# Second MoE: the slot table with 128 columns side by side per chunk

## The chip, the cores and the metric

The kernel runs on one core of one Trainium2 chip. The metric is the device time in microseconds (us) of one launch. The instructions run on five engines: TensorE (PE; its weight loads are listed apart as PEld), VectorE (DVE), ScalarE (ACT), GpSimd (POOL) and SyncE (SP). Each engine takes its own instructions strictly in the order of its queue.

## The reference

The program is banded attention with a linear bias, then a first mixture of experts (MoE) that sends each token to one expert, then a second MoE. What the change touches belongs to the second:

```python
def _moe2_ref(x, w_gate, w1, w2):
    N, D = x.shape                 # 3072, 512
    E = w_gate.shape[1]            # 8
    cap = N // E                   # 384
    logits = x @ w_gate
    order = np.argsort(-logits.flatten())
    assigned = -np.ones(N, dtype=np.int64)
    counts = np.zeros(E, dtype=np.int64)
    for idx in order:
        tok, e = (int(idx) // E, int(idx) % E)
        if assigned[tok] >= 0 or counts[e] >= cap:
            continue
        assigned[tok] = e
        counts[e] += 1
    ...
    for e in range(E):
        mask = assigned == e
        out[mask] = np.maximum(x[mask] @ w1[e], 0.0) @ w2[e]
```

w1 is 512 x 1024 and w2 1024 x 512 for each expert. Each expert ends with exactly 384 tokens.

## The kernel before

Products in fp32 are made of three matmuls in fp32r on high and low parts: high x high, high x low, low x high. So each weight and each activation has a high part (names ending in h) and a low one (ending in l). In the second MoE w1 is wbh and wbl, w2 is wah and wal; xh and xl are the transposed tokens, hh and hl the hidden layer. The high parts of the weights are made on ACT (L119), the low ones on DVE (L121), each chunk of w1 as a pair of two 512-wide halves, four pairs in all, and the same for w2.

The second MoE has eight phases (`phase`, from L1079). Phase i finds the next expert that fills up and its 384 tokens:

- It walks through six digits of the sorted key, DIGITS = 64, 32, 32, 64, 64, 32. For each digit DVE compares (`count`, geT, L1123), PE sums the 0/1 table (`pick`, cg, L1134; 12 matmuls for a digit of 64, 6 for one of 32), DVE copies (cgz, L1136), PE folds (cp, L1141), DVE compares (flz, L1144), PE spreads the result over the partitions (`spread`, fp, L1150), and DVE counts (fo, L1152) and sets up the next digit (db, yk, L1156).
- It numbers the tokens that were found: the matmuls cs (L1229) and spx (L1232, L1241), then on DVE acc, sg and sm. A token's number is split into a column (col) and a row (rw, L1269).
- Four comparisons of 768 elements (L1271) make the 0/1 table `slots` of 128 rows by 24 chunks of tokens, bm and br (L1274 to L1277) make the right side, and 24 matmuls `ip` (L1281), each with one chunk's 128 rows as its stationary matrix, yield the list of tokens: icp (L1283), idx (L1285).

In `slots` the chunk is the innermost index: the 128 elements that one ip takes lie 24 f16 numbers apart.

While phase i+1 runs, expert i is computed. `weights` loads w1 as soon as the expert's number is known (SP, L116, then L119 and L121). `tokens` gathers the tokens through idx into XB (POOL, L1321) and transposes them on PE in three blocks (L151), from which come xh on ACT (L154) and xl on DVE (L155). `ffns` does layer 1 (hp, L175; hh on ACT L179, hl on DVE L180), 96 matmuls of 384 columns, then layer 2 (yp, L207), 72 matmuls of 512 columns, yo on ACT (L1359) and the scatter to the output.

The order on PE is written by `merge`: every generator yields a cost (in columns, 2.4 to the ns) and `merge` takes a matmul from `ffns` until the other generators' cost is used up. So `yield 6000` between the table and ip puts 6000 units of hp or yp there. `phases` multiplies each cost by 1.04 (0.9 in the first phase). The order on DVE, ACT and POOL is set by the compiler's scheduler.

```python
    def phases():
        yield 10000
        for i in range(E):
            while i and -2 not in done1:
                yield 100
            for w in phase(i, found[i]):
                yield (1.04 if i else 0.9) * w
```

Of the kernel before, what the change touches and what calls it, by code (L numbers as in the profile page):

```python
# [12 lines left out]
F16 = mybir.dt.float16  # L13
I32 = mybir.dt.int32
AF = mybir.ActivationFunctionType
OP = mybir.AluOpType
# [13 lines left out]
def attention_moe_moe_kernel(  # L30
# [17 lines left out]
    nc = tc.nc  # L48
# [207 lines left out]
    with ExitStack() as actx:  # L256
# [68 lines left out]
        if not dense:  # L325
# [11 lines left out]
            if n_global:  # L337
                nc.vector.memset(dist[:, G0:G0 + n_global], float(n_local))
                nc.vector.tensor_scalar(dist[:, 256:256 + n_global], dist[:, 256:256 + n_global], float(n_local), None,
                                        op0=OP.min)  # L340
# [230 lines left out]
        for n in range(B * NP):  # L571
            b, hp = divmod(n, NP)
# [66 lines left out]
            if n >= B * NP - 9 and not dense:  # L639
                c = n - (B * NP - 9)  # L640
# [53 lines left out]
    sm1 = ctx.enter_context(tc.tile_pool(name="sm1", bufs=1))  # L694
# [71 lines left out]
    NC_ = N // 128  # L766
# [249 lines left out]
    sel = ctx.enter_context(tc.tile_pool(name="sel", bufs=1))  # L1016
# [6 lines left out]
    for n in (32, 64):  # L1023
# [9 lines left out]
    above = sel.tile([E, 2, 32], F32)  # L1033
    nc.gpsimd.iota(above, pattern=[[1, 2], [1, 32]], base=0, channel_multiplier=0,
                   allow_small_or_imprecise_dtypes=True)
    slots = sm1.tile([128, 2, 128, NC_], F16, name="slots", tag="slots")
    slot16, ao = slots[:, 0], slots[:, 1]
    nc.gpsimd.iota(slot16, pattern=[[1, 128], [0, NC_]], base=0, channel_multiplier=0,
                   allow_small_or_imprecise_dtypes=True)
    pc = sel.tile([128, 1], F32)  # L1040
    nc.gpsimd.iota(pc, pattern=[[1, 1]], base=0, channel_multiplier=1, allow_small_or_imprecise_dtypes=True)
# [32 lines left out]
    def bc(ap, n):  # L1074
        return ap[:, :, None].to_broadcast([128, ap.shape[1], n])
# [4 lines left out]
    def phase(i, found):  # L1080
# [17 lines left out]
        else:  # L1098
# [63 lines left out]
            for a_, sh in enumerate((10, 4, 0)):  # L1162
                nc.vector.tensor_scalar(ki[:, 3 + a_], key, 0xFFFF, sh, op0=OP.bitwise_and,
                                        op1=OP.logical_shift_right)
# [39 lines left out]
            for i_ in range(2):  # L1204
                cx = sel.tile([E, 32], F32, name="cx")
                nc.vector.scalar_tensor_tensor(cx, above[:, i_], dgs[0:E, 5:6], cp[:, :32], op0=OP.is_equal,
                                               op1=OP.mult, accum_out=ct[:, i_:i_ + 1])
            nc.vector.scalar_tensor_tensor(fdz[0:E], ct[:, 1:2].to_broadcast([E, E]), rem8, dcode,
                                           op0=OP.is_ge, op1=OP.mult)
# [51 lines left out]
        sm = sel.tile([128, NC_], F32, name="sm")  # L1261
        nc.vector.tensor_add(sm, sg[:, 0], sg[:, 1])
        nc.vector.tensor_scalar(sm, sm, -1.0, None, op0=OP.add)
        col = sel.tile([128, NC_], F32, name="col")
        nc.vector.tensor_scalar(col, sm, 128.0, None, op0=OP.is_ge)
        for i_ in range(2, NB2):
            nc.vector.scalar_tensor_tensor(col, sm, 128.0 * i_, col, op0=OP.is_ge, op1=OP.add)
        rw = sel.tile([128, NC_], F16, name="rw")
        nc.vector.scalar_tensor_tensor(rw, col, -128.0, sm, op0=OP.mult, op1=OP.add)  # L1269
        for r0 in range(0, 128, 32):  # L1270
            nc.vector.tensor_tensor(ao[:, r0:r0 + 32], slot16[:, r0:r0 + 32],  # L1271
                                    rw[:, None, :].to_broadcast([128, 32, NC_]), op=OP.is_equal)
        bm = sel.tile([128, NC_, NB2], F16, name="bm")
        nc.vector.tensor_tensor(bm, bc(col, NB2), colv[:, None, :].to_broadcast([128, NC_, NB2]), op=OP.is_equal)  # L1274
        br = sel.tile([128, NC_, 2, NB2], F16, name="br")
        nc.vector.tensor_scalar(br[:, :, 0], bm, pc, None, op0=OP.mult)
        nc.vector.tensor_mul(br[:, :, 1], bm, bc(cv, NB2))  # L1277
        yield 6000
        ip = ps.tile([128, 2, NB2], F32, name="ip", tag="sp")
        for c in range(NC_):  # L1280
            nc.tensor.matmul(ip, ao[:, :, c], br[:, c], start=(c == 0), stop=(c == NC_ - 1))  # L1281
        icp = sel.tile([128, NB2], F32, name="icp")
        nc.vector.tensor_copy(icp, ip[:, 1])  # L1283
        idx = sel.tile([128, NB2], I32, name="idx", bufs=E)
# [7 lines left out]
# [7 lines that stand above are left out]
# [98 lines left out]
```

## Time and profile before

| | |
|---|---|
| median of 3 runs | 985.92 us |
| lowest and highest | 983.97 and 986.55 us |
| the profiled execution's own time | 986.66 us |
| its span in the profile | 984.9 us |
| mean granted clock of PE | 0.979 |
| busy: PE, DVE, ACT, POOL | 94%, 56%, 43%, 30% |

The span runs from the first to the last instruction of the profiled execution; the time of the execution holds 1.8 us more. The second MoE fills the last third. Its phases end with ip at 625, 669, 712, 755, 799, 842, 884 and 901 us, so a period of the steady part lasts some 43 us. The phase that ends at 712 us is phase 2, counted from 0.

### The profile page before, as it was taken

The numbers are of one execution on the slowest core, as the hardware profiler recorded it, in microseconds if no ns is written. First come the engines' busy times: TensorE is split into PE (matmuls) and PEld (weight loads), VectorE is DVE, ScalarE is ACT, GpSimd is POOL, SyncE is SP. The second block draws the span as 40 slices with busy tenths as digits, with TensorE's granted clock in tenths as the row PEclk, the third lists the DMA queues.
The fourth block names the chain that finished last, engine by engine and source line by source line (L and its number), as shares of the span: only waits on it lengthen the run. The fifth ranks groups of instructions, "written<-read, shape, count | busy, mean of one in ns | idle before, by whom it ended". The sixth has DMA issues, their size and how long they took to land.

```text
span 984.9 us, 17460 instructions
## 1 busy us (share of the span) xinstructions
PE 927.5 (94%) x6253; PEld 773.4 (79%) x6253; DVE 556.2 (56%) x1928; ACT 424.5 (43%) x939; POOL 298.5 (30%) x272
## 2 busy tenths in 40 slices
PE   7999999999987999999999989689999999998997
PEld 6877777776886899899797756587868787787996
DVE  6657676676232443433334345877878688784530
ACT  5887878875233433334234320134333333432430
POOL 3111534241135465463623871301020210103001
PEclk9999999999998999999999999889999999998999
DMA  8999855630364446544441411515244261524510
GB/s 162 203 200 198 209 140 140 135 124 33 97 195 168 147 134 203 154 141 126 143 150 65 129 52 42 207 51 204 97 150 150 87 213 48 201 101 165 177 39 32
DMA packets 124192, 133.24 MB, mean 135 GB/s; under 512 B 83445, under 2 KB 83585, under 8 KB 124097
## 3 DMA queue, kind: packets, MB, share of 16 engines
q1 hardware_dynamic: 114449, 105.96, 38.6%
q0 software_dynamic: 9648, 26.09, 8.2%
q8 instruction: 51, 0.84, 0.4%
q14 instruction: 44, 0.36, 0.1%
HBM read 103.77 MB, written 28.23 MB: 134 GB/s over the span
## 4 chain that ended last, share of the span: by engine, by line
PE 47%; DVE 8%; issue 7%; DMA 5%; POOL 3%; ACT 1%; POOLq 0%; ACTq 0%; SPq 0%; DVEq 0%
PE hp L175 21%; PE yp L207 12%; PE yp L191 7%; DMA raw<-in_moe_w_dram 4%; DVE wal L121 4%; PE hp L151 2%; PE ip L1281 1%; POOL lg_dram L86 1%; POOL wbl L121 1%; PE cg L1134 1%; DVE geT L1123 1%; DMA XB<-x_dram,idx 1%; ACT wah L119 1%; DVE wbl L121 1%; POOL out_dram L86 1%
## 5 line engine op out<-in xcount | busy, mean ns | idle before, releaser
L179 ACT ACTIVATE hh<-hp 128x384 fp32r<-128x384 f32 (+9 forms) x130 | 63.4, 489 | 186.8 <-PE hp L175 173.1
L180 DVE SCALAR_TENSOR_TENSOR hl<-hp,hh 128x384 fp32r<-128x384 f32 (+9 forms) x130 | 71.8, 554 | 112.5 <-ACT hh L179 112.1
L86 POOL DMA_INDIRECT out_dram<-yo,idx x24 | 26.2, 1091 | 255.1 <-ACT yo L1359 227.1
L121 POOL TENSOR_TENSOR wbl<-raw,wbh 128x1024 fp32r<-128x1024 f32 x28 | 66.4, 2388 | 95.8 <-ACT wbh L119 55.8
L458 ACT ACTIVATE pb<-pb,mn 128x232 f32<-128x232 f32 (+1 forms) x192 | 88.8, 465 | 15.1 <-DVE mn L456 14.5
L207 PE MATMUL yp<-wah,hh 128*128 128x512 f32 x224 | 93.0, 415 | 0.0
L121 DVE TENSOR_TENSOR wal<-raw,wah 128x512 fp32r<-128x512 f32 (+1 forms) x78 | 67.4, 903 | 45.0 <-ACT wah L119 44.5
L119 ACT ACTIVATE wbh<-raw 128x1024 fp32r<-128x1024 f32 x60 | 62.7, 1058 | 69.1 <-DMA raw<-in_moe_w_dram 64.8
L207 PE MATMUL yp<-wah,hl 128*128 128x512 f32 x224 | 91.8, 410 | 0.0
L207 PE MATMUL yp<-wal,hh 128*128 128x512 f32 x224 | 91.4, 408 | 0.0
L444 PE MATMUL sc<-kx,qd 128*128 128x232 f32 (+1 forms) x384 | 88.7, 355 | 2.5 <-POOL kx L420 1.3
L175 PE MATMUL hp<-xl,wah 128*128 128x240 f32 (+8 forms) x260 | 90.9, 349 | 0.0
L175 PE MATMUL hp<-xh,wah 128*128 128x240 f32 (+8 forms) x260 | 90.1, 346 | 0.4 <-PEq L835 0.4
L175 PE MATMUL hp<-xh,wbh 128*128 128x384 f32 (+1 forms) x260 | 90.0, 346 | 0.0
L175 PE MATMUL hp<-xh,wal 128*128 128x240 f32 (+8 forms) x260 | 89.8, 346 | 0.0
L119 ACT ACTIVATE wah<-raw 128x1024 fp32r<-128x1024 f32 x68 | 68.6, 1052 | 48.4 <-DMA raw<-in_moe_w_dram 46.9
L175 PE MATMUL hp<-xh,wbl 128*128 128x384 f32 (+1 forms) x260 | 89.4, 344 | 0.0
L175 PE MATMUL hp<-xl,wbh 128*128 128x384 f32 (+1 forms) x260 | 89.4, 344 | 0.0
L456 DVE CUSTOM_DVE_ANT_0 pb<-sc,bias_w 128x232 f32<-128x232 f32 x160 | 56.7, 393 | 32.3 <-PE sc L444 18.5
L444 PEld LDWEIGHTS sc<-kx,qd 128*128 128x128 f32 x384 | 64.3, 194 | 10.1 <-POOL kx L420 2.4
L121 POOL TENSOR_TENSOR wal<-raw,wah 128x1024 fp32r<-128x1024 f32 x22 | 58.2, 2658 | 42.2 <-ACT wah L119 27.1
L191 PE MATMUL yp<-hh,wbh 128*128 128x240 f32 (+5 forms) x192 | 65.5, 341 | 3.1 <-ACT yt L197 2.1
(307 smaller groups left out, 2140.7 us busy)
## 6 DMA issues: line engine op xcount, KB each, us to landing
raw<-in_moe_w_dram SPq DMA_DIRECT2D x128, 512.0 KB
xs_dram<-qd SPq DMA_DIRECT2D x8, 1032.0 KB
vn<-in_v_dram SPq DMA_DIRECT2D x32, 192.0 KB
kn<-in_k_dram SPq DMA_DIRECT2D x30, 192.0 KB
qn<-in_q_dram SPq DMA_DIRECT2D x30, 192.0 KB
rawg<-in_moe_w_dram SPq DMA_DIRECT2D x8, 512.0 KB
XB<-xs_dram SPq DMA_DIRECT2D x9, 241.9 KB
XB<-xs_dram SPq DMA_DIRECT2D x7, 258.0 KB
```

The lines of the kernel that those rows point to most:

```text
L86: st = nc.gpsimd.indirect_dma_start(out=dst, out_offset=bass.IndirectOffsetOnAxis(ap=idx, axis=0), in_=src, in_offset=None)
L119: nc.scalar.activation(hi, raw, AF.Copy)
L121: lo_engine.tensor_tensor(lo[:, c], raw[:, c], hi[:, c], op=OP.subtract)
L151: tr = nc.tensor.transpose(tp[:, kk], rows[:, kk * 128:(kk + 1) * 128], ident[0:nt, 0:nt])
L175: nc.tensor.matmul(hp_[:, :m], a[:, c], b_[:, kk, t], start=(i == 0), stop=(i == 3 * KD - 1))
L179: nc.scalar.activation(hh[:, t], hp_[:, :m], AF.Relu)
L180: nc.vector.scalar_tensor_tensor(hl[:, t], hp_[:, :m], 0.0, hh[:, t], op0=OP.max, op1=OP.subtract)
L191: nc.tensor.matmul(yp, a[:, c], b_[:, :n], start=(f == 0 and i == 0), stop=(f == KF - 1 and i == 2))
L207: last_mm[0] = nc.tensor.matmul(yp, a[:, c], b_, start=(f == 0 and i == 0), stop=(f == KF - 1 and i == 2))
L444: nc.tensor.matmul(sc[:, h, off:], lhs, kx[:, t, off:], start=True, stop=True)
L456: nc.vector.tensor_tensor_reduce(p[:, h, off:], sc[:, h, off:], bt, 1.0, 3.0e38, OP.add, OP.min, mn)
L458: nc.scalar.activation(p[:, h, off:], p[:, h, off:], AF.Exp, bias=mn, scale=-1.0, accum_out=sums[:, t, hh:hh + 1])
```

## The change

`slots` becomes [128, 24 chunks, 8, 16]: for each chunk 128 columns side by side. The table of row numbers slot16 now holds 128 numbers (it held 128 x 24). rw is written with each row number repeated 16 times, 384 numbers in place of 24, and the comparison, still 4 instructions of 768 elements, runs over 6 chunks at a time in runs of 16 elements. ip takes its 128 columns from one contiguous stretch. The cost that is yielded ahead of ip goes from 6000 to 6500.

```diff
--- before.py
+++ after.py
@@ -1033,9 +1033,10 @@
     above = sel.tile([E, 2, 32], F32)
     nc.gpsimd.iota(above, pattern=[[1, 2], [1, 32]], base=0, channel_multiplier=0,
                    allow_small_or_imprecise_dtypes=True)
-    slots = sm1.tile([128, 2, 128, NC_], F16, name="slots", tag="slots")
-    slot16, ao = slots[:, 0], slots[:, 1]
-    nc.gpsimd.iota(slot16, pattern=[[1, 128], [0, NC_]], base=0, channel_multiplier=0,
+
+    ao = sm1.tile([128, NC_, 8, 16], F16, name="slots", tag="slots")
+    slot16 = sel.tile([128, 8, 16], F16, name="slot16")
+    nc.gpsimd.iota(slot16, pattern=[[16, 8], [1, 16]], base=0, channel_multiplier=0,
                    allow_small_or_imprecise_dtypes=True)
     pc = sel.tile([128, 1], F32)
     nc.gpsimd.iota(pc, pattern=[[1, 1]], base=0, channel_multiplier=1, allow_small_or_imprecise_dtypes=True)
@@ -1265,20 +1266,21 @@
         nc.vector.tensor_scalar(col, sm, 128.0, None, op0=OP.is_ge)
         for i_ in range(2, NB2):
             nc.vector.scalar_tensor_tensor(col, sm, 128.0 * i_, col, op0=OP.is_ge, op1=OP.add)
-        rw = sel.tile([128, NC_], F16, name="rw")
-        nc.vector.scalar_tensor_tensor(rw, col, -128.0, sm, op0=OP.mult, op1=OP.add)
-        for r0 in range(0, 128, 32):
-            nc.vector.tensor_tensor(ao[:, r0:r0 + 32], slot16[:, r0:r0 + 32],
-                                    rw[:, None, :].to_broadcast([128, 32, NC_]), op=OP.is_equal)
+        rw = sel.tile([128, NC_, 16], F16, name="rw")
+        nc.vector.scalar_tensor_tensor(rw, bc(col, 16), -128.0, bc(sm, 16), op0=OP.mult, op1=OP.add)
+        for c0 in range(0, NC_, 6):
+            cs_ = [128, 6, 8, 16]
+            nc.vector.tensor_tensor(ao[:, c0:c0 + 6], slot16[:, None].to_broadcast(cs_),
+                                    rw[:, c0:c0 + 6, None, :].to_broadcast(cs_), op=OP.is_equal)
         bm = sel.tile([128, NC_, NB2], F16, name="bm")
         nc.vector.tensor_tensor(bm, bc(col, NB2), colv[:, None, :].to_broadcast([128, NC_, NB2]), op=OP.is_equal)
         br = sel.tile([128, NC_, 2, NB2], F16, name="br")
         nc.vector.tensor_scalar(br[:, :, 0], bm, pc, None, op0=OP.mult)
         nc.vector.tensor_mul(br[:, :, 1], bm, bc(cv, NB2))
-        yield 6000
+        yield 6500
         ip = ps.tile([128, 2, NB2], F32, name="ip", tag="sp")
         for c in range(NC_):
-            nc.tensor.matmul(ip, ao[:, :, c], br[:, c], start=(c == 0), stop=(c == NC_ - 1))
+            nc.tensor.matmul(ip, ao[:, c].rearrange("p a b -> p (a b)"), br[:, c], start=(c == 0), stop=(c == NC_ - 1))
         icp = sel.tile([128, NB2], F32, name="icp")
         nc.vector.tensor_copy(icp, ip[:, 1])
         idx = sel.tile([128, NB2], I32, name="idx", bufs=E)
```

Lines of the changed kernel are one higher behind the first piece, and two higher behind ip.

The changed cost moves instructions. On PE, each later phase stands some 640 units later against layers 1 and 2: ip of phases 1 to 6 comes behind 9, 12, 15, 18, 21 and 22 yp of layer 2, where it came behind 6 each time. The transposes of the next expert's last block have 10, 7, 7, 4, 1 and 0 yp behind them before layer 1 begins (13 each time before). ACT's order moves behind stage 5 and 6 (wah behind yo and xh). SP's stays. DVE's moves at three places of each phase.

DVE in phase 4, the end of the slot table (slots are the comparisons, br the right side of ip). Before:

```order
L1274 TENSOR_TENSOR bm<-col,colv 128x72
L1114 TENSOR_SCALAR ki<-ki 128x24
L1161 TENSOR_SCALAR ki<-ki 128x24
L1115 TENSOR_REDUCE cmx<-eqb 128x24
L1161 TENSOR_SCALAR ki<-ki 128x24
L1271 TENSOR_TENSOR slots<-slots,rw 128x768 x4
L1276 TENSOR_SCALAR br<-bm,pc 128x24x3
L1277 TENSOR_TENSOR br<-bm,cv 128x24x3
```

And in the changed kernel:

```order
L1276 TENSOR_TENSOR bm<-col,colv 128x72
L1115 TENSOR_SCALAR ki<-ki 128x24
L1162 TENSOR_SCALAR ki<-ki 128x24
L121 TENSOR_TENSOR wbl_10395<-raw,wbh_10394 128x512 x2
L1116 TENSOR_REDUCE cmx<-eqb 128x24
L1162 TENSOR_SCALAR ki<-ki 128x24
L1164 TENSOR_SCALAR ki<-ki 128x24 x3
L1273 TENSOR_TENSOR slots<-slot_7652,rw 128x768 x3
L180 SCALAR_TENSOR_TENSOR hl_10365<-hp,hh_10364 128x384
L1273 TENSOR_TENSOR slots<-slot_7652,rw 128x768
L1278 TENSOR_SCALAR br<-bm,pc 128x24x3
L1279 TENSOR_TENSOR br<-bm,cv 128x24x3
```

The first pair of wbl, three ki and an hl have come to stand ahead of br.

DVE in phase 4, between br and the first digit's geT. Before:

```order
L1116 TENSOR_SCALAR db<-ki 128x24
L1163 TENSOR_SCALAR ki<-ki 128x24
L180 SCALAR_TENSOR_TENSOR hl_10347<-hp,hh_10346 128x384
L1117 TENSOR_TENSOR ohb<-codeb,cmx 128x192
L1163 TENSOR_SCALAR ki<-ki 128x24 x2
L121 TENSOR_TENSOR wbl_10394<-raw,wbh_10393 128x512 x2
L121 TENSOR_TENSOR wbl_10401<-raw,wbh_10400 128x512 x2
L1123 TENSOR_TENSOR geT<-db,jt_7643 128x1536
L121 TENSOR_TENSOR wbl_10408<-raw,wbh_10407 128x512 x2
L180 SCALAR_TENSOR_TENSOR hl_10364<-hp,hh_10363 128x384
L1165 CAST kf<-ki 128x120
```

And in the changed kernel:

```order
L121 TENSOR_TENSOR wbl_10402<-raw,wbh_10401 128x512 x2
L1117 TENSOR_SCALAR db<-ki 128x24
L1118 TENSOR_TENSOR ohb<-codeb,cmx 128x192
L1166 CAST kf<-ki 128x120
L121 TENSOR_TENSOR wbl_10409<-raw,wbh_10408 128x512 x2
L121 TENSOR_TENSOR wbl_10416<-raw,wbh_10415 128x512 x2
L1285 COPY icp<-ip 128x3
L1124 TENSOR_TENSOR geT<-db,jt_7643 128x1536
L1167 TENSOR_SCALAR yk<-kf 128x24
```

Ahead of geT there are now three pairs of wbl, kf and icp behind br, where two pairs and an hl stood.

DVE behind phase 4's table, from the last block's xl to the digit's second geT, where the low parts of w2 (wal) are made. Before:

```order
L155 TENSOR_TENSOR xl<-hp,xh 128x4x128
L121 TENSOR_TENSOR wal_10691<-raw,wah_10690 128x512 x2
L1136 CAST cgz<-cg 128x2x8
L121 TENSOR_TENSOR wal_10698<-raw,wah_10697 128x512 x2
L1144 TENSOR_SCALAR flz<-cp,rem_7680 8x64
L121 TENSOR_TENSOR wal_10705<-raw,wah_10704 128x512 x2
L1152 SCALAR_TENSOR_TENSOR fo,dgs<-fp,onef 128x64
L121 TENSOR_TENSOR wal_10712<-raw,wah_10711 128x512 x2
L1156 SCALAR_TENSOR_TENSOR db<-dgs,yk 128x24
L1156 SCALAR_TENSOR_TENSOR yk<-dgs,yk 128x24
L1123 TENSOR_TENSOR geT<-db,jt_7643 128x1536
L180 SCALAR_TENSOR_TENSOR hl_10717<-hp,hh_10716 128x384
```

And in the changed kernel:

```order
L155 TENSOR_TENSOR xl<-hp,xh 128x4x128
L121 TENSOR_TENSOR wal_10666<-raw,wah_10665 128x512 x2
L121 TENSOR_TENSOR wal_10673<-raw,wah_10672 128x512 x2
L1137 CAST cgz<-cg 128x2x8
L121 TENSOR_TENSOR wal_10680<-raw,wah_10679 128x512 x2
L1145 TENSOR_SCALAR flz<-cp,rem_7681 8x64
L121 TENSOR_TENSOR wal_10687<-raw,wah_10686 128x512 x2
L180 SCALAR_TENSOR_TENSOR hl_10692<-hp,hh_10691 128x384
L1153 SCALAR_TENSOR_TENSOR fo,dgs<-fp,onef 128x64
L1157 SCALAR_TENSOR_TENSOR db<-dgs,yk 128x24
L1157 SCALAR_TENSOR_TENSOR yk<-dgs,yk 128x24
L1124 TENSOR_TENSOR geT<-db,jt_7643 128x1536
```

cgz stands behind two pairs of wal, where it stood behind one, and an hl stands ahead of fo and geT. Behind the tables of phases 1 to 3 an hl stands ahead of geT as well; behind that of phase 5 cgz stands behind three pairs.

At the end of expert 5's layer 2, before, five yp stand between two blocks of transposes on PE and thirteen behind the last; in the changed kernel five and two, and layer 1 of expert 6 follows the last at once.

## Rows read from the trace of the kernel before

**Rows 1.** The page, part 1: busy time of an engine, its share of the span, instructions.

```profile
PE 927.5 (94%) x6253; PEld 773.4 (79%) x6253; DVE 556.2 (56%) x1928; ACT 424.5 (43%) x939; POOL 298.5 (30%) x272
```

**Rows 2.** Windows, one period: us, busy PE, PEld, DVE, ACT, POOL (x), PEclk, DMA, GB/s.

```profile
743.00:786.00 43.00, 40.97 (x283) 33.44 (x282) 33.62 (x128) 14.74 (x22) 6.32 (x6) 1.00 0.41 136
```

**Rows 3.** The chain of waits, 704 to 756 us: start, us, what.

```profile
712.26 1.66 PE ip L1281 x24
713.93 3.60 PE yp L207 x15
717.53 0.30 PE cg L1134 x12
...
729.21 0.44 PE hp L151 x4
...
731.26 0.39 DVE wal L121
...
737.83 0.46 PE cg L1134 x12
```

**Rows 4.** PE's waits, 668 to 870 us: who for whom, us in total, times, longest.

```profile
PE cg L1134 <- DVE geT L1123: 4.3, 5, 0.9
...
PE cp L1141 <- DVE cgz L1136: 1.6, 5, 0.3
```

**Rows 5.** Timeline of PE, phases 2 and 3: start, us, instruction, x count [idle <- releaser].

```profile
705.21 0.20 PE L1241 MATMUL spx<-before,csb 128*128 128x48 f16 x1
...
718.64 0.23 PE L1141 MATMUL cp<-fold,cgz 128*128 128x64 f16 x2
...
748.08 0.20 PE L1241 MATMUL spx<-before,csb 128*128 128x48 f16 x1
```

**Rows 6.** Timeline of DVE, phase 2 and the wal stretch behind it.

```profile
708.84 1.96 DVE L1271 TENSOR_TENSOR slots<-slots,rw 128x768 f16<-128x768 f16 x4
...
710.86 0.24 DVE L1277 TENSOR_TENSOR br<-bm,cv 128x72 f16<-128x72 f16 x1
...
712.06 2.49 DVE L121 TENSOR_TENSOR wbl<-raw,wbh 128x512 fp32r<-128x512 f32 x4
714.47 0.95 DVE L1123 TENSOR_TENSOR geT<-db,jt 128x1536 bf16<-128x1536 bf16 x1
...
730.35 0.69 DVE L155 TENSOR_TENSOR xl<-hp,xh 128x512 fp32r<-128x512 f32 x1
```

**Rows 7.** Groups of weight loads, 600 to 930 us: busy us, mean ns, idle before.

```profile
L1281 PEld LDWEIGHTS <-slots 128*128 128x128 f16 x192 | 13.9, 183 | 2.2 <-issue 1.9 <-DVE ki L1163 0.3
L1134 PEld LDWEIGHTS <-geT 128*128 128x128 bf16 x360 | 11.9, 97 | 17.7 <-DVE geT L1123 9.9 <-issue 4.8 <-DVE xl L155 1.4
```

**Rows 8.** Groups of DVE by form, 600 to 930 us.

```profile
L180 DVE SCALAR_TENSOR_TENSOR hl<-hp,hh 128x384 fp32r<-128x384 f32 x54 | 29.6, 549 | 8.7 <-ACT hh L179 8.6
...
L1271 DVE TENSOR_TENSOR slots<-slots,rw 128x768 f16<-128x768 f16 x32 | 15.6, 551 | 0.0
...
L1123 DVE TENSOR_TENSOR geT<-db,jt 128x768 bf16<-128x768 bf16 x20 | 11.2, 558 | 0.0
...
L1269 DVE SCALAR_TENSOR_TENSOR rw<-col,sm 128x24 f16<-128x24 f32 x8 | 1.4, 177 | 0.0
```

**Rows 9.** Timeline of SP's queue and of ACT where w1 is loaded.

```profile
619.49 12.70 SPq L116 DMA_DIRECT2D raw<-in_moe_w_dram  x8
...
623.30 1.06 ACT L119 ACTIVATE wbh<-raw 128x1024 fp32r<-128x1024 f32 x1 [36.48 <-DMA raw<-in_moe_w_dram]
...
747.64 14.21 SPq L116 DMA_DIRECT2D raw<-in_moe_w_dram  x8
```

**Rows 10.** Windows (as rows 2) and PE's timeline behind a long wait.

```profile
890.00:892.00 2.00, 2.00 (x6) 1.29 (x7) 0.08 (x1) 0.00 (x0) 1.18 (x2) 0.50 0.71 241
...
889.73 0.20 PE L1232 MATMUL spx<-stz,before 128*128 128x48 f16 x1 [2.67 <-DVE csb L1234]
...
890.33 0.63 PE L207 MATMUL yp<-wah,hl 128*128 128x512 f32 x1
```

## The prediction

> **What bounds the kernel now.** The page comes first: TensorE (PE) is busy for 94% of the span [rows 1]. That is a mean over stages, so the second view is one period of the second MoE: PE is busy for 40.97 of 43 us there, VectorE (DVE) for 33.62 [rows 2]. The third view is the chain of waits over the same period [rows 3]. It runs on PE up to 731.24 us, then for 6.5 us over DVE, along the low parts of w2 (wal) with the digit search between them, and back to PE at 737.83 with the table product cg. The fourth view, PE's waits over five periods, agrees: each time PE waits 0.9 us for geT and 0.3 for cgz [rows 4]. So a period is PE's work, plus a microsecond or so in which DVE's first-in-first-out queue is late. Two things count: what the change takes off PE, and whether it makes DVE late where it now just arrives in time.
>
> I count from the product spx at 705.21 us [rows 5], with which the slot table begins. PE is at ip at +7.05 and at the 12 matmuls cg at +12.3 [rows 3], and at cp at +13.4 [rows 5]. DVE writes the last br from +5.65 [rows 6], 1.2 us before ip can use it. Its geT starts at +9.26 and is done at +10.2 [rows 6], **2.1 us before cg needs it**.
>
> **What the change takes away.** The 24 ip matmuls hold PE for 1.66 us of the chain [rows 3]. Each takes its 128 columns out of a table in which they lie 48 bytes apart, and their weight loads last 183 ns; those of cg, whose columns lie side by side, last 97 ns [rows 7]. The twelve cg take 0.30 us [rows 3], so 24 such matmuls would take 0.60. The ends are 0.60 and, by the ratio of the loads, 1.66 x 97/183 = 0.88 us; I take 0.65, nearer to the row of whole matmuls. **PE is relieved of 1.0 us in each of 8 phases, 8.0 in all.** The Trainium skill speaks against that: TensorE: Matmul & The Clock Gate, section Weight-path perf modes — Fast Weight Load (FWL) and DoubleRow, has the fast load on whenever there are 128 weights of a type other than FP32, and ip has 128 of f16 in both kernels. By that rule ip would stay at 1.66 us, and the sum below would be 1 us higher, since only the last phase lets the gain through; rival A would fall away. The loads of 183 and 97 ns disagree with the rule.
>
> **What it adds.** rw grows from 24 to 384 numbers. The nearest row of 384 is hl with 549 ns against rw's 177 [rows 8]: **0.37 us more on DVE** in each phase (ends: nothing, if sixteen equal numbers came cheap, and 0.6). The comparison keeps its 4 x 768 elements. Its runs shrink from 24 elements to 16; geT, of 768 elements in runs of 4, takes 558 ns against 551 [rows 8], so nothing is added (ends -0.05 and +0.05 each). The smaller table of row numbers is filled by GpSimd long before its first use and costs nothing; were it late, it would show in the first comparison alone.
>
> **What it moves.** A yield of 6500 for 6000, times 1.04, shifts every later phase by 520 units against the layers, over and over, and the compiled orders follow. At phase 4 DVE now has the first pair of wbl ahead of cmx and the slots, and all four pairs, an hl and kf ahead of geT; before, two pairs and none ahead of the slots. From spx:
> - SP issues w1 0.4 us before spx (747.64 against 748.08) [rows 5, 9]. From issue to the first conversion is 623.30 - 619.49 = 3.8 us and the conversion takes 1.06 [rows 9]. So the first chunk is ready for DVE at -0.4 + 3.8 + 1.06 = +4.4; its pair of wbl, by 2.49 us for four [rows 6], ends at +5.7.
> - cmx and four ki take some 0.65 (at 0.1 to 0.26 each), the slots 4 x 0.47 (1.96 us for four, less the overlap [rows 6]), hl 0.47, two br 0.3: the last br is done at +9.0. PE stands at ip from +7.05 to +9.0, does it in 0.65, and 15 yp later is at cg at +13.2.
> - DVE meanwhile: a pair 1.25, db, ohb and kf 0.5, two pairs 2.5, geT 0.9: +14.15. **cg comes at +14.2 instead of +12.3: +1.9.** That PE was quicker at ip is lost in the wait.
>
> The other phases by the same steps:
> - Phase 0 is held by DVE from end to end: rw and two yk, **+0.5**.
> - Phases 1 and 2: no early wbl, but rw 0.37, one pair 1.25, hl 0.47 and kf 0.13 stand ahead of geT, 2.2 in all, which uses up the 2.1. Behind geT cgz waits for the last pair: **+0.6** at cp, each.
> - Phase 3 as phase 4, with hl behind the table: **+1.55**. Phase 5: **+1.6**.
> - The wal stretch [rows 3]: in phases 1 to 4 hl moves ahead of geT, **+0.47** each. In phase 5 cgz stands behind three pairs instead of one, so flz, hl and fo lose their cover: hl 0.47, the trips of flz and fo to PE and back, twice the 0.23 us that cp takes there [rows 5], and an xh behind a yo on ScalarE, 0.6 if it is as long as xl: **+1.6**.
> - Stage 6: thirteen yp stood between the last transposes and layer 1, now none. The transposes end at 729.65 in the period shown [rows 3] and xl at 731.04 [rows 6]: 1.4 us idle. With 0.4 of wait ahead of it and ip of phase 7 at -1.0: **+0.8**.
>
> **Sum:** 0.5 + 2 x (0.6 + 0.47) + (1.55 + 0.47) + (1.9 + 0.47) + (1.6 + 1.6) + 0.8 = **+11.0 us**. The profiled execution took 986.66 us, which makes 997.7; it lies 0.74 above the median of 985.92, so **997.0**. A change under 0.3%, 2.96 us, cannot be told from none, so the bounds are 983.0 and 988.9. My own range comes from the ends: rw at nothing takes off 7 x 0.37 = 2.6 and w1 landing 1 us earlier in three phases 3, so 991; ip at 0.88, w1 0.7 us later in three phases and another 1.4 at phase 5 add 4 to 5, so 1002.
>
> **Rivals.** *A, PE-bound throughout (faster).* If DVE's lateness doesn't reach PE, the 8.0 us remain: 978. For it speak PE's 94% [rows 1]; against it, that geT is already waited for in every period [rows 4] and that its 2.1 us must hold 2.2 more on DVE and the 1.0 by which PE comes earlier. It decides where fewer than two things move ahead of geT, or w1 lands before DVE has come to the slots. The Trainium skill (Perfetto Trace Analysis, section Identifying the Most-Contended Engine) says to relieve the engine with the highest occupancy first, which would have this rival win; that the chain leaves PE for 6.5 us in a period disagrees. Chance 0.14, with those cases in which part of the gain is eaten.
>
> *B, gain and delay cancel (same).* If ScalarE has the first chunk ready before DVE gets there, and hl has slack, phases 1 to 5 lose 0.2 each, phase 0 0.5, and stage 6 and 7 come out at -0.6: +0.9, 987. Chance 0.12.
>
> *C, the forecast with a lower clock (slower still).* A wait of 2.67 us is followed by a stretch in which the granted clock is 0.50 (1.2 instead of 2.4 GHz) and a yp takes 0.43 us [rows 10], where 15 take 3.6 at the full one [rows 3]: 13 of them lose 2.5. The waits of 2 us at ip and 1 at cg in phases 3 to 5 come near that; three times 2.5 is 7.5 more, 1005. Waits of 0.9 us have no such stretch behind them in the period, whose clock is 1.00 [rows 2]. Chance 0.14.
>
> *The forecast*, 991 to 1002: 0.60. **Chances:** faster 0.14, same 0.12, slower 0.60 + 0.14 = 0.74. With 2 in 10 left out, most of A and the top of C, the range goes from 984 to 1006.
>
> **What the changed profile would show.** ip in about 0.65 us with weight loads near 97 ns; rw at some 549 ns; the comparison still at 551. In phase 4 PE idle for 2 us ahead of ip, released by br, and for another 1 ahead of cg; a pair of wbl just ahead of the slots. PE's waits for geT over the five periods well over the 4.3 us of before [rows 4]. Ahead of expert 6's first hp 1.4 us idle. I am wrong if the first chunk is ready for DVE before +3.2 in phase 4, so that the slots aren't late, if geT ends before +11.3, or if ip's loads stay at 183 ns.

## Result and profile after

The changed kernel takes **990.91 us** (median of 8 runs, 988.8 to 993.31) against 984.29 us (8 runs, 981.99 to 986.55) on the same chip: ratio 1.0067, 95% interval 1.005 to 1.0083, so **slower by 6.6 us**. The forecast was 997.0 in a range of 984 to 1006, and slower. The profiled execution took 991.54 us, its span is 989.8 (984.9 before).

What the change says of itself holds. The page and the groups by form of the changed kernel, 600 to 935 us (columns as in [rows 1, 7, 8]; from the comparison on, lines are two higher than before):

```profile
PE 922.3 (93%) x6253; PEld 765.7 (77%) x6253; DVE 558.9 (56%) x1928; ACT 424.2 (43%) x939; POOL 304.5 (31%) x272
```

```profile
L1135 PEld LDWEIGHTS <-geT 128*128 128x128 bf16 x358 | 11.8, 97 | 20.9 <-DVE geT L1124 15.2 <-issue 5.0 <-DVE xl L155 0.6
L1283 PEld LDWEIGHTS <-slots 128*128 128x128 f16 x192 | 5.3, 96 | 6.6 <-DVE br L1279 5.8 <-issue 0.5 <-DVE kf L1166 0.3
```

```profile
L1273 DVE TENSOR_TENSOR slots<-slot,rw 128x768 f16<-128x768 f16 x32 | 15.8, 550 | 0.0
...
L1270 DVE SCALAR_TENSOR_TENSOR rw<-col,sm 128x384 f16<-128x384 f32 x8 | 4.4, 552 | 0.0
```

A weight load of ip takes 96 ns instead of 183 [rows 7], as one of cg does; the 24 matmuls of ip hold PE for 0.62 us, from one start to that of the next instruction, where they stood for 1.66 us in the chain [rows 3]. rw costs 552 ns instead of 177, the comparison what it did [rows 8]. PE is busy 5.2 us less, and the span is 4.9 us longer: PE waits more. Its waits, 668 to 870 us, beside [rows 4]:

```profile
PE cg L1135 <- DVE geT L1124: 5.7, 7, 1.2
PE ip L1283 <- DVE br L1279: 2.8, 3, 1.3
PE cp L1142 <- DVE cgz L1137: 2.1, 5, 0.9
PE fp L1151 <- DVE flz L1145: 1.5, 4, 0.4
PE hp L175 <- DVE xl L155: 1.3, 3, 0.7
PE hp L175 <- ACT xh L154: 1.2, 2, 0.8
```

ip, xl and xh had no wait before. Over the whole second MoE, 600 us to the end, the listed waits grow from 21.0 to 32.0 us, by 11.0; ip saves 8 x 1.05 = 8.4. The difference is 2.6 of the 4.9 us; the other 2.3 are in nothing that this view lists.

Where it happens is seen in one period, phase 4. First PE's timeline there, then DVE's:

```profile
794.77 0.20 PE L1242 MATMUL spx<-before,csb 128*128 128x48 f16 x1
...
803.89 0.76 PE L1283 MATMUL ip<-br,slots 128*128 128x6 f16 x24 [1.34 <-DVE br L1279]
...
808.91 0.46 PE L1135 MATMUL cg<-ohb,geT 128*128 128x16 bf16 x12 [0.67 <-DVE geT L1124]
```

```profile
797.66 0.55 DVE L1270 SCALAR_TENSOR_TENSOR rw<-col,sm 128x384 f16<-128x384 f32 x1
...
799.31 1.30 DVE L121 TENSOR_TENSOR wbl<-raw,wbh 128x512 fp32r<-128x512 f32 x2 [0.79 <-ACT wbh L119]
...
801.11 1.49 DVE L1273 TENSOR_TENSOR slots<-slot,rw 128x768 f16<-128x768 f16 x3
...
803.60 0.24 DVE L1279 TENSOR_TENSOR br<-bm,cv 128x72 f16<-128x72 f16 x1
803.74 1.29 DVE L121 TENSOR_TENSOR wbl<-raw,wbh 128x512 fp32r<-128x512 f32 x2
...
805.42 2.49 DVE L121 TENSOR_TENSOR wbl<-raw,wbh 128x512 fp32r<-128x512 f32 x4
...
807.90 0.95 DVE L1124 TENSOR_TENSOR geT<-db,jt 128x1536 bf16<-128x1536 bf16 x1
```

DVE stands for 0.79 us at a pair of wbl that ScalarE hasn't converted yet, with the slots queued behind it; then three pairs more go ahead of geT. The chain of waits, which in [rows 3] ran over PE in this stretch, now runs over ACT's wbh and over DVE, through wbl and the slots to geT, and meets PE at cg:

```profile
797.75 0.48 DVE rw L1270
798.23 1.06 ACT wbh L119
799.31 1.30 DVE wbl L121 x2
...
801.20 1.40 DVE slots L1273 x3
...
805.51 2.41 DVE wbl L121 x4
807.99 0.88 DVE geT L1124
808.91 0.46 PE cg L1135 x12
```

That rw released wbh is inferred by the profile, and not likely: wbh starts 3.88 us after SP issued the load of w1 here, and 3.65 to 4.44 us after it in phases 1 to 6, where the profile names other instructions or the transfer itself. More likely ACT waits for the weights, and DVE for ACT.

### The profile page after: what moved, and what is told of

The parts are those of the page before. It is cut to its first block, busy times and chain, and to the rows that moved or that the text cites. A ratio compares the mean times of both kernels' runs of the same rounds, so it can differ in the third digit from the quotient of the medians.

```text
span 989.8 us, 17442 instructions
## 1 busy us (share of the span) xinstructions
PE 922.3 (93%) x6253; PEld 765.7 (77%) x6253; DVE 558.9 (56%) x1928; ACT 424.2 (43%) x939; POOL 304.5 (31%) x272
## 4 chain that ended last, share of the span: by engine, by line
PE 40%; DVE 15%; issue 8%; DMA 5%; POOL 3%; ACT 2%; POOLq 0%; SPq 0%; ACTq 0%; DVEq 0%
PE hp L175 18%; PE yp L207 9%; PE yp L191 7%; DMA raw<-in_moe_w_dram 4%; DVE wal L121 3%; DVE wbl L121 3%; PE hp L151 2%; DVE geT L1124 1%; DVE slots L1273 1%; DVE hl L180 1%; POOL lg_dram L86 1%; POOL wbl L121 1%; PE cg L1135 1%; ACT wah L119 1%; ACT wbh L119 1%
## 5 line engine op out<-in xcount | busy, mean ns | idle before, releaser
L86 POOL DMA_INDIRECT out_dram<-yo,idx x24 | 33.4, 1390 | 278.3 <-ACT yo L1361 251.7
```

Of the source, the lines that this page charges most:

```text
L86: st = nc.gpsimd.indirect_dma_start(out=dst, out_offset=bass.IndirectOffsetOnAxis(ap=idx, axis=0), in_=src, in_offset=None)
```

## Experiments

The theory of the experiments is this. PE's gain at ip is real, and is lost because DVE's queue has the low parts of w1 (wbl) ahead of what PE waits for (slots, geT, cgz). Rival 1 is that the shift by the cost 6500 is the loss (transposes without cover), rival 2 that only the longer rw costs. Each ratio is against the kernel before on the same chip. The chips differ: the kernel before took 993.3, 996.6 and 996.8 us on those of the three groups below.

**The two halves of the change by themselves.** The new table with the old cost:

```diff
-        yield 6500
+        yield 6000
```

> The new table with the old cost 6000 ahead of ip, so the order on PE is that of before. Theory (the low parts of w1 stand ahead of geT and cgz on DVE): ip 0.62 us, but geT ends at about +12.4 after spx in phases 1 to 5 and cp comes at about +14.0 where it came at +13.4; 0.6 to 0.9 us lost in each of five phases, nothing in phase 0, 1.0 gained at the last: +2 to +3.5 us, ratio 1.002 to 1.0035. Rival 1 (the shift by 6500 is the whole loss): the 8 us of ip appear in full, 0.992. Rival 2 (only the longer rw costs): 8 less 2.6 us, 0.9945.

Measured: 1.0064 (1.0049 to 1.0079). And the old table with the new cost, the same edit the other way:

> The table of before with cost 6500 ahead of ip, nothing else. PE's order is that of the changed kernel, ip stays at 1.66 us. Theory: PE comes 0.5 us later to cg, which gives DVE slack in phases 1 and 2 (no wait for geT there); in phases 3 to 5 a pair of wbl ahead of the slots makes ip and cg wait 0.5 to 1.2 us, and the last transposes go uncovered, 1 us: +2 to +4 us, ratio 1.002 to 1.004. Rival 1 (the shift is the whole loss): +14 us, the loss of the change without its gain, 1.014. Rival 2: 1.000.

Measured: 1.0052 (1.0032 to 1.0072). Rival 1 and rival 2 both fall with the first run: PE's order is there that of before, and it is as slow as the whole change. The direction is the theory's, the size isn't: both halves cost more than forecast, and together (1.0067, on the chip of the result) they cost hardly more than each alone. The places do agree. DVE and PE in phase 2 of the run with cost 6000:

```profile
719.31 3.69 DVE L121 TENSOR_TENSOR wbl<-raw,wbh 128x512 fp32r<-128x512 f32 x6
...
723.39 0.94 DVE L1124 TENSOR_TENSOR geT<-db,jt 128x1536 bf16<-128x1536 bf16 x1
```

```profile
711.94 0.20 PE L1242 MATMUL spx<-before,csb 128*128 128x48 f16 x1
...
724.39 0.46 PE L1135 MATMUL cg<-ohb,geT 128*128 128x16 bf16 x12 [1.06 <-DVE geT L1124]
...
725.97 0.23 PE L1142 MATMUL cp<-fold,cgz 128*128 128x64 f16 x2 [0.33 <-DVE cgz L1137]
```

cg comes at +12.45 after spx and cp at +14.03, where PE's timeline of before has them at +12.16 and +13.43: the microsecond that ip gave has become a wait of 1.06, and 0.6 more is lost at cp. In the run with cost 6500 alone, phase 3 has the same picture as the change's phase 4, a wait of 0.68 us of a wbl for wbh ahead of the slots and one of 0.64 of ip for br.

**Moving wbl on DVE.** The low parts of w1 are handed out by code: two pairs are queued behind the next phase's first geT, one behind its second, one behind its third. The orders of PE, ACT and GpSimd are those of the run with cost 6000; on DVE, wbl apart, a cgz, icp or hl moves past a neighbour. (`later` holds the low parts that are not issued yet, `counts` the geT of each phase and digit; of this edit and those below only the lines that hand out are shown.)

```diff
+                for r, n_ in ((0, 2), (1, 1), (2, 1)):
+                    while (i + 1, r) not in counts:
+                        yield 100
+                    with tc.issue_after(counts[i + 1, r].ins):
+                        for _ in range(n_):
+                            later.pop(0)()
```

> The new table with cost 6000; the low parts of w1 are issued behind the next phase's digits: two pairs of wbl behind the first geT, one behind the second, one behind the third. Theory: geT ends at +8.8, cg waits for nothing and comes at +11.2, cp at +12.4, one us earlier than before; phases 1 to 5 gain 1.0 us each, the last 1.0, phase 0, which DVE bounds, 1 to 2: ratio 0.991 to 0.993. Rival 1: as its forecast for the run with cost 6000, 0.992 for both, so no difference between the two runs. Rival 2: 0.9945.

Measured: 0.9972 (0.9954 to 0.9991). The same edit on the kernel before:

> The table of before with the low parts of w1 issued behind the next phase's digits as in the run above. Theory: before, geT and cgz were just in time in phases 1 to 5, so nothing is gained there; phase 0 gains 1 to 2 us: ratio 0.998 to 0.999, and the difference to the run above is ip's 1.0 us in each phase. Rival (the order of wbl costs the same under either table): a gain as large as that between the two runs with the new table, 0.99.

Measured: 1.0012 (0.9991 to 1.0032). This pair bears the theory out: under the new table the order of wbl is worth 0.9972 - 1.0064, 8 to 9 us; under the old one nothing. The size was missed again, -2.8 where -7 to -9 us was forecast, and the two runs differ by 0.0040, half of the 8 us that the second expectation gives to ip. cg does come at +11.2 without a wait, and cp at +12.3 to +13.3, but part of the gain is handed on. PE in phase 3 of that run, and its waits from 870 us on:

```profile
755.85 0.20 PE L1249 MATMUL spx<-before,csb 128*128 128x48 f16 x1
...
767.08 0.46 PE L1142 MATMUL cg<-ohb,geT 128*128 128x16 bf16 x12
768.40 0.23 PE L1149 MATMUL cp<-fold,cgz 128*128 128x64 f16 x2
...
777.17 0.66 PE L158 MATMUL hp<-ident,XB 128*128 128x128 f32 x4 [1.80 <-DMA XB<-x_dram,idx]
```

```profile
PE spx L1240 <- DVE csb L1242: 4.2, 1, 4.2
```

In phase 3, and of the five there alone, the transposes wait for the gathered tokens, whose list idx stands behind the same wbl in DVE's queue. (The kernel before waits 0.5 us at this place, with idx at +13.4 after spx and the transposes at +20.9; here they are at +12.4 and +21.3. So idx is not later than it was: PE is ready 0.9 us sooner, and what follows idx takes longer.) Near the end spx waits longer for csb, which stands behind expert 6's wbl.

**Moving idx and csb ahead too.** wbl is queued behind idx as well, and expert 6's behind the last phase's br:

```diff
-                    with tc.issue_after(counts[i + 1, r].ins):
+                    with tc.issue_after(counts[i + 1, r].ins), tc.issue_after(idxs[i].ins):
...
+            if i == E - 2:
+                while (i + 1, 7) not in counts:
+                    yield 100
+                with tc.issue_after(counts[i + 1, 7].ins):
+                    while later:
+                        later.pop(0)()
```

> The new table with cost 6000 and the low parts of w1 behind the next phase's digits, as in the run before; they now stand behind idx as well, and those of expert 6 behind the last phase's br. Theory (the gain of the run before was handed on to waits for the gathered tokens XB, whose idx stood behind wbl, and for csb behind wbl in the last phase but one): idx at about +9 after spx in place of +13.2, no wait of the transposes for XB, no wait of spx for csb and no lower clock behind it: 4 to 8 us less than the run before, ratio 0.986 to 0.991. Rival (the gain stops because XB is late by its own transfer, whatever idx does): transposes at +20.9 after spx as before, 0.995 to 0.998.

Measured: **0.9897** (0.9863 to 0.9931), as forecast; the rival falls. idx runs at +9.4 to +10.4 after spx in phases 1 to 5, where it ran at +12.0 to +13.2 in the run before this one. PE's waits, 668 to 870 us:

```profile
PE cg L1142 <- DVE geT L1131: 3.4, 4, 0.9
PE cp L1149 <- DVE cgz L1144: 2.2, 6, 0.6
PE fp L1158 <- DVE flz L1152: 1.8, 5, 0.4
```

The wait for XB is gone, and that for csb (0.5 us are left at that spx, behind idx). The gain over the run before is thus not spread over the digits. The profiled spans are 981.6 and 989.2 us; counted from the first yp of one expert to that of the next, 2.2 us of the difference lie in phase 3, where XB was late, and 5.1 between experts 5 and 6 (37.10 instead of 42.19 us), where the wait of 4.2 us for csb was followed by some 3 us at 1.2 GHz. The kernel before has a wait there too, of 2.3 us on this chip. Against its profile on this chip, further down, the five periods of the digits give 5.7 us, this one stretch, in which ip runs twice, 5.4, and what lies ahead of them 2.0. So a good part of the gain comes from a wait that was there before the change.

**Handing out w2's low parts as well.** A pair of wal each behind the digits 4, 5 and 6 and one behind the phase's last comparison, by a generator of its own (`later2` holds the low parts of w2):

```diff
+    def lows():
+        for i in range(E - 2):
+            while i not in ready:
+                yield 100
+            for r, n_ in ((3, 1), (4, 1), (5, 1), (6, 1)):
+                while (i + 1, r) not in counts:
+                    yield 100
+                with tc.issue_after(counts[i + 1, r].ins):
+                    for _ in range(n_):
+                        later2.pop(0)()
```

> As the run with idx and br ahead of w1's low parts, and the low parts of w2 handed out too: one pair of wal behind each of the digits 4, 5 and 6 and one behind the last comparison of the phase. Theory: the waits of 0.9 us for geT, 0.3 for cgz and 0.4 for flz in the wal stretch go in each of five phases, 5 to 7 us: ratio 0.980 to 0.986. Rival (PE or the loads bound there, and wal was cover): the ratio of the run without it, to 0.002.

Measured: 0.9886 (0.985 to 0.9921), 0.001 from the run without it: the forecast failed. The waits of the wal stretch go, and as much comes back at the phase's end, where fdz now stands behind a pair of wal. PE's waits, 668 to 870 us:

```profile
PE fb L1224 <- DVE fdz L1216: 4.2, 5, 0.9
PE cp L1149 <- DVE cgz L1144: 2.6, 7, 0.8
```

The same order with the old table, and the kernel before on this chip:

> The table of before with the same order of the low parts of w1 and w2 as the run above. Theory: with DVE out of the way PE bounds, so the two differ by what ip takes less, 1.05 us in 7 or 8 phases: this run is 6 to 8 us slower than the one above, ratio 0.987 to 0.993. Rival (DVE's queue still bounds): the two are equal within 2 us.

> The kernel before, for a profile on the same chip: any theory expects 1.000, and the waits of rows 4.

Measured: 0.9905 (0.9876 to 0.9934) and 996.52 us. What the table itself is worth under this order, 0.0019 or 2.7 us by the medians, is within the intervals and less than the 6 to 8 us forecast. PE's waits for cgz are 2.6 us with the new table, as shown above, and 1.6 with the old:

```profile
PE cp L1148 <- DVE cgz L1143: 1.6, 5, 0.3
```

The periods from first yp to first yp show where ip's gain gets through. With the old table all five take 42.35 us. With the new one they take 41.44 in the two in which the first cp behind ip doesn't wait for cgz, 41.63 and 41.80 where it waits 0.06 and 0.22 us, and 42.40 where it waits 0.81. So 0.9 of ip's 1.05 us reach the period where DVE is in time, and a late cgz takes them back. The profile of the kernel before shows that chip's 10 us ahead of the second MoE's steady part: expert 0's first hp comes at 656.7 instead of 645.6 us, and cg and cp stand at +12.2 and +13.4 as ever.

**What remained open: the size.** The change and the run with cost 6000 on one chip, each with a second profile:

> The changed kernel beside the runs below, on their chip. Theory (what the cost 6500 moves on PE is worth nothing, the order of wbl on DVE everything): 1.005 to 1.008, and the run with cost 6000 within 0.003 of it. Rival (the shift itself costs): over 0.003 slower than the run with cost 6000.

> The new table with cost 6000 a second time. Theory: cgz at +13.8 after spx in phases 1 to 5 and cp at +14.0, 0.6 us later than before, the wait for geT in the wal stretch as before, idx 0.4 us later, which now and then makes the transposes wait for XB: 1.003 to 1.008. Rival (the first run fell on a disturbed stretch, the loss is the 2.5 us of cp and cg alone): 1.0005 to 1.003.

Measured: 1.0095 (1.0064 to 1.0127) for the change, above its forecast, and 1.0073 (1.0044 to 1.0102) with cost 6000, within its own. The two lie within 0.003, as the theory has it, and the intervals don't exclude that the shift costs a little. The expected later transposes are there in the second profile (+22.4 and +22.8 in phases 3 and 5 against +20.87 in the others), but XB isn't why. Windows around cg and cp of phase 5, columns as in [rows 2], and PE's timeline:

```profile
844.00:858.00 14.00, 13.83 (x94) 11.76 (x92) 13.66 (x54) 5.78 (x8) 0.00 (x0) 1.00 0.54 184
858.00:861.00 3.00, 1.78 (x19) 1.26 (x20) 2.67 (x9) 0.60 (x1) 0.00 (x0) 1.00 0.83 287
861.00:864.00 3.00, 3.00 (x10) 2.02 (x9) 1.10 (x6) 0.00 (x0) 2.28 (x3) 0.51 0.90 288
```

```profile
858.89 0.46 PE L1135 MATMUL cg<-ohb,geT 128*128 128x16 bf16 x12 [1.06 <-DVE geT L1124]
...
860.48 0.23 PE L1142 MATMUL cp<-fold,cgz 128*128 128x64 f16 x2 [0.33 <-DVE cgz L1137]
...
862.23 0.63 PE L207 MATMUL yp<-wal,hh 128*128 128x512 f32 x1
862.66 0.63 PE L207 MATMUL yp<-wah,hl 128*128 128x512 f32 x1
```

After the two waits the granted clock is 0.51 (1.2 instead of 2.4 GHz) for about 3 us, and a yp takes 0.43 us instead of 0.23. The next digit's cg comes at +18.4 after spx, where it comes at +16.9 in the phases without such a stretch: 1.55 us lost. From the first yp of expert 0 to 885 us such stretches occur once or twice in four of the five profiles of the change and its two halves (not in the change's first), twice in the run with geT first and four times in the run with a slow comparison, both below, and in no profile of the kernel before or of the runs above with w1's low parts handed out. They don't all stand behind two waits: in the change's second profile one follows a single wait of 1.49 us ahead of ip, in the run with cost 6500 alone a single one of 0.64 us. So a wait has a second price that isn't paid in every execution. The profiled execution with cost 6000 is the fastest of its six, 5.5 us under their median, so its trace can't show all that the median lost; how much of that is clock was not measured.

**geT first, but not cgz.** All four pairs of wbl queued behind the first geT:

```diff
+                with tc.issue_after(first[i + 1].ins):
+                    while later:
+                        later.pop(0)()
```

> The new table with cost 6000 and all four pairs of wbl behind the first geT, ahead of cgz. Theory (the queue only hands the wait on): cg at +11.2 without a wait, but cgz behind the four pairs at +13.9 and cp at +14.0, as with wbl ahead of geT; phases 1 to 5 no better than in the run with cost 6000: ratio within 0.002 of it. Rival (geT alone is what PE waits for): cp at +12.4 and a gain of 1 us a phase, 0.993 to 0.997.

Measured: 1.0116 (1.0079 to 1.0153). The queue hands the wait on, and more: cg comes at +11.24 without a wait, cp at +14.4 to +15.3. At 0.004 above the run with cost 6000 it is also slower than the theory had it, which forecast a distance of 0.002 at most. Its waits, 668 to 885 us:

```profile
PE cp L1149 <- DVE idx L1295: 8.6, 4, 2.3
PE cp L1149 <- DVE cgz L1144: 5.5, 6, 2.9
```

(DVE's releasing instruction is named idx where that ends less than 0.1 us before cgz.) So geT alone isn't what PE lacks; the rival falls.

**Why rw is written 16 times.** The changed kernel with rw left at 24 numbers:

```diff
-        rw = sel.tile([128, NC_, 16], F16, name="rw")
-        nc.vector.scalar_tensor_tensor(rw, bc(col, 16), -128.0, bc(sm, 16), op0=OP.mult, op1=OP.add)
+        rw = sel.tile([128, NC_], F16, name="rw")
+        nc.vector.scalar_tensor_tensor(rw, col, -128.0, sm, op0=OP.mult, op1=OP.add)
...
-                                    rw[:, c0:c0 + 6, None, :].to_broadcast(cs_), op=OP.is_equal)
+                                    rw[:, c0:c0 + 6, None, None].to_broadcast(cs_), op=OP.is_equal)
```

> The changed kernel with rw left at 24 numbers; the comparison reads each one 16 times over with a step of 0. If the comparison's rate does not depend on the repeated numbers lying in memory: slots stays at 551 ns, rw at 177, 0.37 us a phase less on DVE, ratio 0.996 to 0.999 of the changed kernel. Rival (the step of 0 costs the comparison its rate): slots at about twice 551 ns, 1.9 us more a phase, br at +8 after spx, 8 to 12 us slower than the changed kernel.

Measured: 1.0177 (1.0145 to 1.0209), 7.7 us by the medians above the change on the same chip, just below the 8 to 12 us of the rival's forecast. The groups of DVE by form, 600 to 935 us:

```profile
L1273 DVE TENSOR_TENSOR slots<-slot,rw 128x768 f16<-128x768 f16 x32 | 28.5, 951 | 0.0
...
L1270 DVE SCALAR_TENSOR_TENSOR rw<-col,sm 128x24 f16<-128x24 f32 x8 | 1.4, 177 | 0.0
```

A step of 0 in the innermost place takes the comparison from 551 to 951 ns: 0.37 us saved at rw against 1.6 lost at the slots. Within this table the longer rw is the cheaper choice.

## Why the prediction was right, and where it was off

The direction, its reason and the place of each wait were right; the sum, +11.0 against +4.9 in the profiled execution and +6.6 in the medians, was too large. On the chip of the later runs the change cost some 9.5 us (1.0095). Its profile there has a stretch at the lower clock behind a wait, which the sum doesn't hold, so this nearness is no support for the sum.

**What PE gains, what DVE gets.** ip 0.62 us (0.65 forecast), its loads 96 ns (97), rw 552 ns (549), the comparison 550 (551). The Trainium skill (TensorE: Matmul & The Clock Gate, section Weight-path perf modes — Fast Weight Load (FWL) and DoubleRow) has the fast load on whenever there are 128 weights of a type other than FP32. What the prediction read from it, that ip would stay at 1.66 us, isn't borne out: with 128 weights of f16 in both kernels the load takes 96 ns from side by side and 183 ns from 48 bytes apart. The rule doesn't say that the layout costs nothing, and whether the fast load was on in either kernel no run here shows.

**Where cg comes.** From spx, in us:

| phase | 1 | 2 | 3 | 4 | 5 |
|---|---|---|---|---|---|
| first cg before | 12.16 | 12.16 | 12.17 | 12.17 | 12.17 |
| later by, forecast | 0.1 | 0.1 | 1.55 | 1.9 | 1.6 |
| later by, measured | 0.29 | 0.34 | 1.61 | 1.97 | 1.49 |
| cg of the wal stretch later by, forecast | 1.07 | 1.07 | 2.02 | 2.37 | 3.2 |
| measured | 0.87 | 0.89 | 1.31 | 2.30 | 2.86 |

The working for phase 4 holds on DVE: the first wbh was forecast ready at +4.4, and it ends at 799.28, +4.5; br was forecast done at +9.0 and is done at +9.07, geT at +14.15 and at +14.08.

**The step that missed is the sum itself.** It took every microsecond by which cg is later *from spx* as lost. But the cost 6500 for 6000, times 1.04, puts 0.52 us more of hp and yp between spx and ip in each phase, work that is then missing elsewhere and isn't lost. The prediction named the 520 units and used them for the orders alone. It shows at ip: PE was left at +7.05 there, but it is done with the three more yp ahead of ip at +7.6 in phase 1 and, after twelve more yp and twelve fewer hp, at +7.8 in phase 4. So PE waits 1.34 us ahead of ip and 0.67 ahead of cg in phase 4, where 2 and 1 were forecast. (A unit is a nanosecond of matmul, columns divided by 2.4; the section on the kernel before calls it a column, which is wrong.) Counted at a fixed place in the layers, the first yp of each expert, the periods grow by (the lines are those of experts 4 and 5, before and after):

```profile
839.94 0.39 PE L207 MATMUL yp<-wah,hh 128*128 128x512 f32 x1
...
882.79 0.39 PE L207 MATMUL yp<-wah,hh 128*128 128x512 f32 x1
```

```profile
842.66 0.39 PE L207 MATMUL yp<-wah,hh 128*128 128x512 f32 x1
...
888.02 0.39 PE L207 MATMUL yp<-wah,hh 128*128 128x512 f32 x1
```

| from the first yp of expert | 0 to 1 | 1 to 2 | 2 to 3 | 3 to 4 | 4 to 5 | 5 to 6 |
|---|---|---|---|---|---|---|
| forecast | 1.07 | 1.07 | 2.02 | 2.37 | 3.2 | 0.8 |
| measured | 0.19 | 0.39 | 0.62 | 1.58 | 2.51 | -0.33 |

Five phases were forecast at 9.7 us in all. Measured from spx they come 8.2 us later, and at the yp the sum is 5.3; the 2.9 us between are the moved work, nearly 0.6 a phase. Two smaller terms were off as well. Phase 0 was put at +0.5 and is -0.1 at the first yp. The end was put at +0.8: xh and xl do wait there, 0.8 + 0.3 us in place of 1.4, but spx waits 2.2 us for csb where it waited 2.7.

**What was put at nothing.** The smaller table and the comparison's shorter runs cost nothing that shows. The order of ACT was counted in one place, 0.6 us for an xh behind a yo in phase 5, and the trace has it there: yo starts at 864.86, xh at 865.35, and layer 1 waits 0.79 us for it.

**The rivals.** A, PE-bound, didn't come, and the runs with both low parts handed out show its condition: where no cgz is late, 0.9 us of ip's gain reach the period. With wbl behind idx the new table takes 0.9897; the old one was not run under just that order, and under the longer one it takes 0.9905. The Trainium skill (Perfetto Trace Analysis, section Identifying the Most-Contended Engine) says to optimize the engine with the highest occupancy first, and for TensorE it goes by the share of the peak rate or by the weight loads in place of the busy matmuls. Matmuls and weight loads both have PE first here, 94% and 79% [rows 1]. Taken by itself the rule doesn't say what a relief of that engine is worth: PE was relieved of 8 us, and the kernel got slower, while the order on DVE, busy for 56%, was worth 9 us by the medians under the old table (0.9905). B, cancelling, didn't come: the early wbl did hold up the slots. C, the lower clock, came in part: behind the digits not in the first profile of the change, but in all the other profiles of the slower kernels.

## What to carry to other kernels

A gain on the busiest engine reaches the end only if its partner's queue had slack for it: before shortening a step, look at what its followers on the other engine stand behind, and move independent work (here the low parts of weights for a layer that is still to come) out of that queue's way first. A change to a scheduled program is also a change of order; here the order alone, on one engine, was worth more (9 us with the old table, in part from the wait for csb at the end) than the step that was made faster. And when a change shifts work between two marks, count the loss at a mark that doesn't move against the work.

## What was not expected of the hardware

- A step of 0 in the innermost dimension of one f16 operand takes a comparison of 768 elements from 551 to 951 ns; with the repeats in memory, in runs of 16, it takes 550.
- Waits of 1.06 and 0.33 us, one behind the other, and single ones of 1.49 and 0.64 us were followed by some 3 us at 1.2 GHz. The same two waits stand without it in other phases of the same profiles, and the 0.9 us of [rows 4] have none behind them. The forecast of C expected it behind waits of 2 us ahead of ip and 1 ahead of cg.
